# Attention with learned features beside a Mish feed-forward: weight loads rewritten and a new order of steps

## The chip, the cores and the metric

The kernel runs on one core of one Trainium2 chip. The metric is device time in microseconds (us): the median over runs of the whole kernel. A core has five engines with queues of their own: TensorE (PE, with its weight loads listed as PEld), VectorE (DVE), ScalarE (ACT), GpSimd (POOL) and SyncE (SP). SP issues nearly all transfers here, ACT a few; 16 DMA engines move them.

## The reference

```python
xn = layernorm(x)                                   # x: 1 x 2048 x 448, bf16
q, k, v = split(xn @ wqkv)                          # 16 heads of 28
phi(t) = concat(softmax(t @ w_phi), softmax(-(t @ w_phi)))   # per head, 28 x 28
kv, z = phi(k)^T v, sum over rows of phi(k)
o = (phi(q) kv) / (phi(q) z + 1e-6)
A = o @ wo
h = xn @ w1 + b1                                    # 448 to 1792
B = (h * tanh(softplus(h))) @ w2                    # Mish, then 1792 to 448
out = x + A + B
```

## The kernel before

The 2048 rows are held as 16 tiles of 128; two tiles make a pair `u` (0 to 7). The model width of 448 is three chunks of 128 and a tail of 64. For the tail the two tiles of a pair use the two halves of TensorE's rows at the same time: the normalised input is transposed to `xnT[u]` with the tail of the even tile on partitions 0 to 63 and that of the odd tile on 64 to 127. So each product has a part "F" (six matmuls over the full chunks, two tiles) and a part "H" (two matmuls of 64 rows, one per tile). The weights must therefore stand twice in their chunk 3, once in each half: `W1` (feed-forward) gets its tail by two transfers, `Wv` gets its by two, and `Wk` has its tail in partitions 0 to 63 and zeros (`p_wz`) in 64 to 127.

The feature map is folded into the projections: `Wp[1]` = Wk times w_phi and `Wp[0]` = Wq times w_phi. For this the key weights are transposed on TensorE (`w_tr`, steps wtk0 and wtk1; wtk1 holds the tail), the query weights by transposing transfers (`load_qT`, steps lqT0 to lqT3, with a doubling copy `qd`), and both are multiplied by the block-diagonal `Wbd` (`w_mm`, steps wmk and wmq). `Wbd` is built on GpSimd from the raw features `Wraw` and a 0/1 mask (`p_mask`, `w_bd`).

All work is a list of named steps. `ORDER` says in which order they are entered; each step appends its instructions to the queue of its engine, and each engine runs its own queue in that order, waiting only on what its instruction needs. Names that matter here, with `u` a pair, `t` a tile:

- `lx..`, `lkm`, `lkt`, `lvm`, `lvt`, `lp`, `lb`, `l1m`, `l1t`, `l2`, `lo`: loads of x, of key and value weights (main and tail), of features, bias, W1 (chunks and tail), W2 and Wo; the last letter is the queue (s for SP, a for ACT).
- `st` statistics (VectorE), `rt`/`rs` inverse deviation (ACT or GpSimd), `xm`/`xn` normalisation, `xa`/`xb` the transposition of a pair on TensorE in two parts (only pairs 3 and 1), `xt{u}m` the same by a transposing transfer on SP (the other pairs). An `xt` transfer waits until all of x is loaded.
- `v{u}`, `k{u}`, `q{u}` with F or H: the projections; `exk`, `exq` exponentials on ACT; `kn` and `qn` normalise the softmax (reduction on VectorE, multiplication on GpSimd); `kv{u}` the product of features and values, `kvz` its finish, `e{t}` transposing transfers of the query features.
- `f{half}.{c}` with F or H: first feed-forward product, followed by Mish on ACT; `g{t}` the second; `nd`, `ot`, `wo`, `sto` the attention output, its transposition, its projection and the stores.
- `z10`: ten matmuls on constants at the start.

Results of TensorE go to four pairs of PSUM banks; a pair is written again only when the engine that copies it out is done.

Of the kernel before, what the change touches and what calls it, by code (L numbers as in the profile page):

```python
# [35 lines left out]
def ap_on(src, dims):  # L36
    return bass.AP(tensor=src.tensor, offset=src.offset, ap=[list(src.ap[0])] + [list(d) for d in dims])
# [6 lines left out]
class Program:  # L44
# [46 lines left out]
    def dma(self, eng, fn, r=(), w=(), tag=""):  # L91
        return self.op(eng, fn, r, w, dma=True, tag=tag)
# [64 lines left out]
q5H xn7d k5H v4Ha k4H v4Fd qn6p xt7m l1m0s k4F qn4p q6F k6F v5Ha q6H qn7p qn2p k7H xt0m l1ts e7 k6H v5Fd kn3.0 k7F q7F  # L157
v6Fa q7H kn1.1 kn4.1 kn1.0 q0H qn13p f1.0H v6Ha q0F kn2.1 f1.0F f0.1F f0.5F v0Fd f0.1H f0.5H f1.2H kn3.1 v0Hd f1.2F
f1.5F f1.4H f1.5H k0H kn7.0 kn6.1 kn2.0 v7Hd kn7.1 ep f1.4F k0F v7Fd qn14p q4F f1.3F q4H kn5.1 e6 f0.2H f1.3H f0.0H
kn0.1 f0.2F f0.0F e2 f0.3F e4 kn6.0 kv7 e14 kn5.0 kn0.0 kv1 kv3 f0.9H f0.3H f0.9F los f1.1F kn4.0 f0.13F f0.10F f0.13H  # L160
f1.1H qn11p qn12p kv5 kv0 kv6 kv2 kv4 f0.12H f0.6H f0.10H f0.6F qn3p kvz qn9p f0.12F qn5p f1.6F e3 qn1p f1.6H qn8p
f0.4H f1.10H f0.7H qn0p f1.10F f0.4F nd7 wob e5 qn15p f0.7F nd4 f1.9F f0.11F f1.12F f0.11H f1.12H f1.8H f1.9H f1.8F
# [12 lines left out]
def _kernel(es, nc, A_x, A_wqkv, A_w_phi, A_wo, B_w1, B_b1, B_w2, out):  # L175
    def sb(name, shape, dtype):
        return es.enter_context(nc.sbuf_tensor(name, shape, dtype))
# [4 lines left out]
    ident = sb("ident", [P, P], BF16)  # L182
    mask = sb("mask", [GP, 4], FP32)
    Wraw = sb("Wraw", [GP, G, DH], BF16)
    Wbd = sb("Wbd", [GP, G, 2, 64], BF16)
    mask2 = sb("mask2", [P, 2, 2, DH], FP32)
    b1_rows = sb("b1_rows", [FC, P], BF16)
    b1T = sb("b1T", [P, FC], FP32)
# [50 lines left out]
    home_rows = {"Wk": [("Wk", 0), ("Wt", 0), ("Wt", 1), ("Wz",)], "Wv": [("Wv", 0)], "Wq": [("WqT", g) for g in range(G)] + [("WqTd",)],  # L239
                 "Wp1": [("Wp", 1, h, c) for h in range(2) for c in range(2)]}  # L240
# [22 lines left out]
    def pb(b):  # L263
        return ("ps", b)
# [14 lines left out]

    def load_tail(eng, name, dst, src):  # L280
        for i, (lo, hi) in enumerate(HALF):
            dma(eng, lambda e, lo=lo, hi=hi: e.dma_start(dst[lo:hi, 3, :], src[384:448, :]),
                w=[(name, 1 + i)], tag="ld" + name)

    def load_kv_tail(eng):
        dma(eng, lambda e: e.dma_start(Wkv[0:64, 3, :], A_wqkv[384:448, D:3 * D]), w=[("Wt", 0)], tag="ldWkt")  # L286
# [12 lines left out]
    def rows_of(name):  # L299
        if name in ("Wk", "Wv"):  # L300
            return [(name, 0), ("Wt", 0), ("Wz",) if name == "Wk" else ("Wt", 1)]
        return [("W1", 0, c) for c in range(3)] + [("W1", 1), ("W1", 2)]

    def load_phi(eng):
        dma(eng, lambda e: e.dma_start(Wraw[:], A_w_phi.rearrange("(g j) d f -> (j d) g f", j=4)), w=[("Wraw",)],
            tag="ldWphi")
# [27 lines left out]

    def p_mask():
        op("POOL", lambda e: e.memset(mask[:], 1.0), w=[("mask",)], tag="pm0")
        op("POOL", lambda e: e.affine_select(out=mask[:], in_=mask[:], compare_op=ALU.is_ge, fill=0.0, base=0,
                                             channel_multiplier=1, pattern=[[-DH, 4]]),
           r=[("mask",)], w=[("mask",)], tag="pm1")
        op("POOL", lambda e: e.affine_select(out=mask[:], in_=mask[:], compare_op=ALU.is_ge, fill=0.0, base=DH - 1,  # L340
                                             channel_multiplier=-1, pattern=[[DH, 4]]),
           r=[("mask",)], w=[("mask",)], tag="pm2")

    def p_wbd():
        op("POOL", lambda e: e.memset(Wbd[:], 0.0), w=[("Wbd0",)], tag="pw0")

    def p_wz():
        op("DVE", lambda e: e.memset(Wkv[64:128, 3, 0:D].bitcast(mybir.dt.uint32), 0), w=[("Wz",)], tag="pz0")

# [67 lines left out]
    def pe(fn, r, w, tag):  # L417
        return op("PE", fn, r=r, w=w, tag=tag)
# [173 lines left out]

    def w_bd():
        for r in range(2):
            op("POOL", lambda e, r=r: e.tensor_tensor(
                Wbd[:, :, r, 0:QP].rearrange("p g (j f) -> p g j f", f=DH),
                ap_on(Wraw[:, 0, 0:1], [[DH, G], [0, 2], [1, DH]]),
                ap_on(mask[:, 2 * r:2 * r + 1], [[0, G], [1, 2], [0, DH]]), ALU.mult),
               r=[("Wraw",), ("mask",), ("Wbd0",)], w=[("Wbd", r)], tag=f"Wbd{r}")

    def w_tr(h, eng):
# [27 lines left out]
    def w_mm(which, h, eng):  # L629
# [8 lines left out]
        def mm(e):  # L638
# [4 lines left out]
            return ins  # L643
        pe(mm, ([("WT", h), ("WU", h)] if which else [("WqT", g) for g in range(G)] + [("WqTd",)]) + [("Wbd", 0), ("Wbd", 1)], [pb(b), pb(b + 1)], f"wmm{which}{h}")
        if which and eng == "both":
# [120 lines left out]
    def bias_T():  # L766
        b = take1()
        pe(lambda e: e.transpose(bank16(b)[:, 0:FC], b1_rows[0:FC, :], ident[0:FC, 0:FC]), [("b1r",), ("ident",)],
           [pb(b)], "b1")
        evac("DVE", lambda: b1T[:], lambda: bank16(b)[:, 0:FC], [pb(b)], [("b1T",)], "b1e")  # L770

# [197 lines left out]
    add("table", table)  # L969
    add("bd", w_bd)  # L970
    for eng, c in (("SP", "s"), ("ACT", "a")):
        for name, a, b in (("x0", 0, 2), ("x1", 2, 4), ("x2", 4, 6), ("x3", 6, 8), ("x4", 8, 12), ("x6", 12, 16)):
            add(f"l{name}{c}", load_x, a, b, eng)
        for i, (n, t) in enumerate((("k", Wk), ("v", Wv))):
            add(f"l{n}m{c}", load_main, eng, "W" + n, t, A_wqkv[:, (i + 1) * D:(i + 2) * D])
        add(f"lkt{c}", load_kv_tail, eng)
        add(f"lvt{c}", load_v_tail, eng)
        for i in range(3):
            add(f"l1m{i}{c}", load_chunk, eng, "W1", W1, B_w1, i)
        add(f"l1t{c}", load_tail, eng, "W1", W1, B_w1)  # L980
        for name, fn in (("p", load_phi), ("b", load_b1), ("2", load_w2), ("o", load_wo)):
            add(f"l{name}{c}", fn, eng)
# [62 lines left out]
```

## Time and profile before

| | us |
|---|---|
| median of 3 runs (lowest, highest) | 152.07 (152.03, 152.78) |
| profiled execution | 151.9 |
| its span, first to last instruction | 150.4 |
| TensorE busy | 146.1 (97%) |
| VectorE / ACT / GpSimd busy | 90.3 / 71.4 / 70.4 |

Times inside the profile count from the first instruction of the profiled execution. A row of the chain is "start, duration, what"; a row of the timeline is "start, duration, engine, line, operation, output from input, count"; a row of transfers ends with the size of one transfer and the time from issue to landing. The windows list busy time of PE, PEld, DVE, ACT and POOL with counts, then the granted clock, the busy share of the 16 DMA engines and GB/s. Groups give total busy us and the mean ns of one instruction.

### The profile page before, as it was taken

To read this page: it belongs to the slowest core of one execution; us is meant where nothing else is said; L and a number is where in the kernel's file an instruction comes from. 1 tells how busy PE (TensorE), PEld (TensorE's weight loads), DVE (VectorE), ACT (ScalarE), POOL (GpSimd) and SP (SyncE) were. 2 spreads that over 40 slices of the span, in tenths; PEclk is the share of its full clock that TensorE was granted. 3 is DMA by queue.
4 is the path that set the end of the run, shared out by engine and by line. 5 is a ranking of instruction groups with operands and counts; after the bars stand their busy time and mean duration, and the time that the engine had idled before them with its cause. 6 is when DMAs were issued, how large, how long until landed. Compare 5 with 4: busy or idle time off the path is not lost.

```text
span 150.4 us, 2592 instructions
## 1 busy us (share of the span) xinstructions
PE 146.1 (97%) x1051; PEld 72.3 (48%) x1051; DVE 90.3 (60%) x180; ACT 71.4 (47%) x85; POOL 70.4 (47%) x77
## 2 busy tenths in 40 slices
PE   7899999999999999999999999999999999999992
PEld 2554444444443535454354445555455555554451
DVE  0997996899999899947986004514049351200641
ACT  3688998989986979546681974000000000000000
POOL 7522799399999999998999100000000000000000
PEclk9999999999999999999999999999999999999999
DMA  5997696796830009401479994530905933030206
GB/s 131 271 234 215 127 251 114 142 226 40 174 70 0 0 0 126 162 0 29 80 145 355 155 197 89 101 65 9 188 3 39 256 86 61 0 65 0 92 0 214
DMA packets 39480, 16.97 MB, mean 113 GB/s; under 512 B 33452, under 2 KB 38700, under 8 KB 39468
## 3 DMA queue, kind: packets, MB, share of 16 engines
q1 hardware_dynamic: 38860, 16.68, 51.6%
q10 hardware_dynamic: 608, 0.12, 0.4%
q8 instruction: 8, 0.13, 0.3%
q14 instruction: 4, 0.03, 0.1%
HBM read 6.97 MB, written 1.84 MB: 59 GB/s over the span
## 4 chain that ended last, share of the span: by engine, by line
PE 89%; SPq 5%; DMA 2%; DVE 1%; issue 0%
PE PS L440 49%; PE PS L883 28%; PE PS L899 7%; PE PS L800 2%; DMA WqT<-in_A_wqkv_dram 2%; SPq L292 2%; PE PS L707 2%; SPq L271 1%; SPq L274 1%; PE PS L641 1%; DVE x_all L848 0%; SPq L286 0%; SPq L289 0%; DVE WqT L296 0%; DVE x_all L869 0%
## 5 line engine op out<-in xcount | busy, mean ns | idle before, releaser
L440 PE MATMUL PS<-xnT,W 128*128 128x512 bf16 (+1 forms) x224 | 45.5, 379 | 0.0
L883 PE MATMUL PS<-W,actT 128*128 128x448 bf16 (+1 forms) x224 | 44.0, 351 | 0.0
L774 ACT ACTIVATE actT<-PS,b1T 128x1024 bf16<-128x1024 f32 x28 | 30.1, 1113 | 13.3 <-PE PS L440 13.1
L883 PEld LDWEIGHTS PS<-W,actT 128*128 128x128 bf16 x224 | 21.4, 98 | 18.8
L440 PEld LDWEIGHTS PS<-xnT,W 128*128 128x128 bf16 (+1 forms) x224 | 17.6, 97 | 24.4 <-issue 5.4
L755 POOL TENSOR_TENSOR EqS<-EqS,rSk 128x896 bf16<-128x896 bf16 x16 | 26.7, 1694 | 3.0 <-DVE rSk L753 3.0
L690 POOL TENSOR_TENSOR actT<-actT,rSk 128x896 bf16<-128x896 bf16 x16 | 26.6, 1693 | 0.0
L848 DVE TENSOR_TENSOR x_all<-PS,x_all 128x448 bf16<-128x448 f32 (+1 forms) x16 | 9.5, 617 | 20.8 <-PE PS L899 14.4
L805 DVE RECIPROCAL rden<-PS 128x16 f32<-128x16 f32 x16 | 4.0, 250 | 24.2 <-PE PS L800 24.2
L751 DVE TENSOR_REDUCE Sk<-EqS 128x32 f32<-128x896 bf16 x16 | 16.7, 1042 | 0.0
L686 DVE TENSOR_REDUCE Sk<-actT 128x32 f32<-128x896 bf16 x16 | 16.5, 1033 | 0.0
L740 ACT ACTIVATE EqS<-PS 128x896 bf16<-128x896 f32 x16 | 13.8, 943 | 2.6 <-PE PS L440 2.6
L678 ACT ACTIVATE actT<-PS 128x896 bf16<-128x896 f32 x16 | 13.7, 941 | 0.2 <-PE PS L440 0.2
L440 PE MATMUL PS<-Wkv,xnT 128*128 128x448 bf16 (+1 forms) x64 | 13.2, 353 | 0.0
L440 PE MATMUL PS<-Wpk,xnT 128*128 128x448 bf16 (+1 forms) x64 | 13.0, 353 | 0.0
L440 PE MATMUL PS<-Wpq,xnT 128*128 128x448 bf16 (+1 forms) x64 | 12.5, 353 | 0.0
L472 DVE BATCH_NORM_STATS2 stats<-x_all 128x6 f32<-128x448 bf16 x16 | 9.7, 608 | 2.6 <-DMA x_all<-in_A_x_dram 2.6
L807 DVE TENSOR_TENSOR xn<-PS,rden 128x448 bf16<-128x448 f32 x16 | 10.0, 625 | 0.6
L440 PEld LDWEIGHTS PS<-Wpq,xnT 128*128 128x128 bf16 (+1 forms) x64 | 5.2, 97 | 6.2 <-issue 1.9
L440 PEld LDWEIGHTS PS<-Wkv,xnT 128*128 128x128 bf16 (+1 forms) x64 | 5.0, 97 | 6.0 <-issue 1.9
L440 PEld LDWEIGHTS PS<-Wpk,xnT 128*128 128x128 bf16 (+1 forms) x64 | 5.3, 97 | 5.2 <-issue 0.6
L567 DVE CAST v_all<-PS 128x896 bf16<-128x896 f32 x5 | 5.4, 1079 | 2.3 <-PE PS L440 2.3
(80 smaller groups left out, 108.7 us busy)
## 6 DMA issues: line engine op xcount, KB each, us to landing
W<-in_B_w_dram SPq DMA_DIRECT2D x1, 1568.0 KB, 9.0
out_dram<-x_all SPq DMA_DIRECT2D x7, 224.0 KB, 2.3
W<-in_B_w_dram SPq DMA_DIRECT2D x3, 448.0 KB, 3.9
x_all<-in_A_x_dram SPq DMA_DIRECT2D x4, 224.0 KB, 3.5
x_all<-in_A_x_dram SPq DMA_DIRECT2D x2, 448.0 KB, 4.2
Wkv<-in_A_wqkv_dram SPq DMA_DIRECT2D x2, 336.0 KB, 4.1
Wo<-in_A_wo_dram SPq DMA_DIRECT2D x2, 336.0 KB, 4.0
W<-in_B_w_dram SPq DMA_DIRECT2D x2, 224.0 KB, 4.7
```

The lines of the kernel that those rows point to most:

```text
L440: ins = e.matmul(o, lhs(c, k), rhs(c, k), start=first and c in (0, 3), stop=not first and c in (2, 3))
L472: op("DVE", lambda e: e.bn_stats(stats[:, t, :], x_all[:, t, :]), r=[("x", t)], w=[("st", t)], tag=f"bn{t}")
L678: op("ACT", lambda e, s=s: e.activation(E_of(u)[:, s, :, :], two(b, D), ACT.Exp, scale=1.0 if s == 0 else -1.0), r=[pb(b), pb(b + 1)], w=[ ...
L686: op("DVE", lambda e: e.tensor_reduce(Sk[u][:, s, :], Eh(), AX.X, ALU.add), r=[("E", u, s)], w=[("Sk", u, s)], tag=f"Sk{u}.{s}")
L690: op("POOL", lambda e: e.tensor_tensor(Eh(), Eh(), ap_on(rSk[u][:, s, 0:1], [[1, 2 * H], [0, DH]]), ALU.mult), r=[("E", u, s), ("rSk", u, ...
L740: op("ACT", lambda e, s=s: e.activation(EqS[:, k:k + 2, :, s * QP:(s + 1) * QP], two(b, D).rearrange("p i (h n) -> p i h n", n=QP), ACT.Ex ...
L751: op("DVE", lambda e: e.tensor_reduce(ap_on(Sk[u][:, i, 0:1], [[4, 2 * G], [1, 4]]), E, AX.X, ALU.add), r=both, w=[("Sk", u, i)], tag=f"Sq ...
L755: op(eng, lambda e: e.tensor_tensor(E, E, ap_on(rSk[u][:, i, 0:1], [[4, 2 * G], [1, 4], [0, DH]]), ALU.mult), r=both + [("rSk", u, i)], w= ...
L774: op("ACT", lambda e: e.activation(actT[:, fc, q * 1024:(q + 1) * 1024], bank(b, 2), ACT.Mish, bias=b1T[:, fc:fc + 1]), r=[("b1T",), pb(b) ...
L807: op("DVE", lambda e: e.tensor_tensor(o_sb[u % NXN][:, i, :].rearrange("p (h d) -> p h d", d=DH), ap_on(bank(b)[:, 0:1], [[NC, H], [1, DH] ...
L883: ins = e.matmul(bank(b)[:, 0:width(t)], actT[:, fc, tok(t)], W2[:, fc, 0:width(t)], start=first and fc == 0, stop=last and fc == FC - 1)
L899: ins = e.matmul(bank(b)[:, 0:n], oT_of(u)[lo:hi, cc * P:(cc + 1) * P], Wo[lo:hi, cc, 0:n], start=first and c in (0, 3), stop=last and c i ...
```

## The change

- Features are loaded by four transfers on ACT (lp0 to lp3) directly into their blocks of `Wbd`; `Wraw`, the mask and `w_bd` go. The transfers wait for the memset of `Wbd`.
- The key tail goes into partitions 0 to 63 of `Wk`'s chunk 3 and the value tail into 64 to 127 of the same chunk, in one transfer of 128 rows; the zeros go. `Wv` keeps only the lower half of its own tail, and the products of odd tiles read the value tail from `Wk` (`tok_works` has a `W3`).
- The tail of `W1` is loaded in one transfer whose source names the same 64 rows twice.
- The bias is loaded by columns (`b1_cols`, 128 x 14), and the transposition on TensorE goes; a copy on VectorE makes it fp32.
- A new order. Among other things: x tiles 2 and 3 (lx1s) are loaded ahead of the value weights, tiles 4 and 5 last; wtk1b stands ahead of xa3a; tile 7 is normalised on GpSimd; the W1 tail (l1ts) is issued between xt5m and xt4m; nine constant matmuls instead of ten.

```diff
-pm pw lx3s pk pz lkms lkts lvms lvts lpa table pi lx1s lqT0 lx2s st6d rt6a st7d z10 rt7a lqT1 lx4s lqT2 lqT3 xm6d lx0s
-pv wtk0b lx6s xm7d xa3a wtk1b bd wmk0b xb3a st3d wmk1a st2d v3Fd st5d rt3p rt2a xm2d v3Ha xm3d lbs k3F st4d xa1a k3H
-xb1d v1Fa qd wmq1a rs2p st11d xn2d wmq0a st10d k1F b1 k1H st13d rs5p xn5p v1Ha q1H q3H st9d st12d q1F q3F xt2m q2F k2F
-st8d st0d k2H rs4p v2Hd st1d l1m1s xt5m xn4d rs6p rs0p l1m2s xt4m q2H xn6p st15d st14d v2Fd rs7p xt6m k5F xn0p q5F pp
...
+pw lx3s lkms lkts lx1s lvms lvts lx4s lp1a pi lp0a st6d lqT3 lp2a lqT0 lp3a st7d table rt6a z9 rt7a xm6d wtk0b xm7p
+wtk1b xa3a lqT1 st2d wmk0a rt2p lqT2 st3d xb3d lx0s pk rt3a wmk1a v3Fd xm2d xa1a v3Ha xm3d st10d st11d st8d qd st9d
+k3H rs5p xb1a lx6s k3F v1Fd xn5d lx2s wmq0a wmq1d rs4p v1Ha xn4p pp st15d k1H st14d st5d k1F xt5m l1ts q3F q1F st4d
+xt4m st1d st12d rs2p q1H xn2d rs7p kn1.0 q3H lbs v5Ha k5H k5F xt2m v5Fa q5F v4Fd st0d rs0p st13d xn7d l1m0s q5H rs6p
+v4Hd xn0d q4H q4F k2F xt7m k4F l1m1s pv xn6p k2H k4H v2Hd k7F kn1.1 v2Fa xt0m qn2p kn2.1 q2F xt6m kn4.0 kn2.0 k7H
...
-    def load_tail(eng, name, dst, src):
-        for i, (lo, hi) in enumerate(HALF):
-            dma(eng, lambda e, lo=lo, hi=hi: e.dma_start(dst[lo:hi, 3, :], src[384:448, :]),
-                w=[(name, 1 + i)], tag="ld" + name)
+    def load_w1_tail(eng):
+        src = bass.AP(tensor=B_w1.tensor, offset=B_w1.offset + 384 * F, ap=[[0, 2], [F, 64], [1, F]])
+        dma(eng, lambda e: e.dma_start(W1[:, 3, :], src), w=[("W1", 1)], tag="ldW1")
 
     def load_kv_tail(eng):
-        dma(eng, lambda e: e.dma_start(Wkv[0:64, 3, :], A_wqkv[384:448, D:3 * D]), w=[("Wt", 0)], tag="ldWkt")
+        src = bass.AP(tensor=A_wqkv.tensor, offset=A_wqkv.offset + 384 * 3 * D + D, ap=[[D, 2], [3 * D, 64], [1, D]])
+        dma(eng, lambda e: e.dma_start(Wk[:, 3, :], src), w=[("Wt", 0)], tag="ldWkt")
 
     def load_v_tail(eng):
-        dma(eng, lambda e: e.dma_start(Wkv[64:128, 3, D:2 * D], A_wqkv[384:448, 2 * D:3 * D]), w=[("Wt", 1)], tag="ldWvt")
+        dma(eng, lambda e: e.dma_start(Wv[0:64, 3, :], A_wqkv[384:448, 2 * D:3 * D]), w=[("Wt", 1)], tag="ldWvt")
...
-    def load_phi(eng):
-        dma(eng, lambda e: e.dma_start(Wraw[:], A_w_phi.rearrange("(g j) d f -> (j d) g f", j=4)), w=[("Wraw",)],
-            tag="ldWphi")
+    def load_phi(j, eng):
+        dma(eng, lambda e: e.dma_start(Wbd[j * DH:(j + 1) * DH, :, j // 2, j % 2 * DH:(j % 2 + 1) * DH],
+                                       A_w_phi.rearrange("(g j) d f -> j d g f", j=4)[j]),
+            r=[("Wbd0",)], w=[("Wbd", j)], tag=f"ldWphi{j}")
 
     def load_b1(eng):
-        dma(eng, lambda e: e.dma_start(b1_rows[:], B_b1.rearrange("(c p) -> c p", p=P)), w=[("b1r",)], tag="ldb1")
+        dma(eng, lambda e: e.dma_start(b1_cols[:], B_b1.rearrange("(c p) -> p c", p=P), allow_slow_non_contiguous=True), w=[("b1r",)], tag="ldb1")
...
-    def w_bd():
...
     def bias_T():
-        b = take1()
-        pe(lambda e: e.transpose(bank16(b)[:, 0:FC], b1_rows[0:FC, :], ident[0:FC, 0:FC]), [("b1r",), ("ident",)],
-           [pb(b)], "b1")
-        evac("DVE", lambda: b1T[:], lambda: bank16(b)[:, 0:FC], [pb(b)], [("b1T",)], "b1e")
+        op("DVE", lambda e: e.tensor_copy(b1T[:], b1_cols[:]), r=[("b1r",)], w=[("b1T",)], tag="b1e")
```

More of the change, by code (lines that the diff above doesn't have):

```diff
@@ L158 @@
[L158 to L162, printed above, removed]
@@ L167 @@
+nd12 wob g0 ot5m e0 g1 nd14 nd0 ot0m g13 ot7m wo5F ot6m g4 g12 g10 g14 wo7F wo6F wo0H wo7H wo6H wo5H wo0F sto6 g11
+sto2 sto0 sto3 g15 sto1 stt14 sto4 sto5 stt15
 """
@@ L182, in _kernel @@
     ident = sb("ident", [P, P], BF16)
-    mask = sb("mask", [GP, 4], FP32)
-    Wraw = sb("Wraw", [GP, G, DH], BF16)
     Wbd = sb("Wbd", [GP, G, 2, 64], BF16)
     mask2 = sb("mask2", [P, 2, 2, DH], FP32)
-    b1_rows = sb("b1_rows", [FC, P], BF16)
+    b1_cols = sb("b1_cols", [P, FC], BF16)
     b1T = sb("b1T", [P, FC], FP32)
@@ L238, in _kernel @@
     oT_home = [(Wkv, 0, ["Wk", "Wv"]), (Wkv, 14 * P, []), (WqT, 0, ["Wq"]), (Wp[1], 0, ["Wp1"])]
-    home_rows = {"Wk": [("Wk", 0), ("Wt", 0), ("Wt", 1), ("Wz",)], "Wv": [("Wv", 0)], "Wq": [("WqT", g) for g in range(G)] + [("WqTd",)],
+    home_rows = {"Wk": [("Wk", 0), ("Wt", 0), ("Wt", 1)], "Wv": [("Wv", 0)], "Wq": [("WqT", g) for g in range(G)] + [("WqTd",)],
                  "Wp1": [("Wp", 1, h, c) for h in range(2) for c in range(2)]}
@@ L333, in p_ident @@
            r=[("ident",)], w=[("ident",)], tag="pi1")
[L335 to L342, printed above, removed]
     def p_wbd():
         op("POOL", lambda e: e.memset(Wbd[:], 0.0), w=[("Wbd0",)], tag="pw0")
-    def p_wz():
-        op("DVE", lambda e: e.memset(Wkv[64:128, 3, 0:D].bitcast(mybir.dt.uint32), 0), w=[("Wz",)], tag="pz0")
     def p_ones():
@@ L589, in xT @@
              [("xnT", u), ("xnU", u)], f"xTe{u}")
-    def w_bd():
[L594 to L599, printed above, removed]
     def w_tr(h, eng):
@@ L643, in mm @@
             return ins
-        pe(mm, ([("WT", h), ("WU", h)] if which else [("WqT", g) for g in range(G)] + [("WqTd",)]) + [("Wbd", 0), ("Wbd", 1)], [pb(b), pb(b + 1)], f"wmm{which}{h}")
+        pe(mm, ([("WT", h), ("WU", h)] if which else [("WqT", g) for g in range(G)] + [("WqTd",)]) + [("Wbd", j) for j in range(4)], [pb(b), pb(b + 1)], f"wmm{which}{h}")
         if which and eng == "both":
@@ L662, in xchunk, with tok_works @@
         return c if c == 3 or par == 0 else 4 + c
-    def tok_works(u, W):
+    def tok_works(u, W, W3=None):
         return lambda b: [(bank(b + par)[:, 0:D], par,
                            lambda c, k, par=par: xnT[k[0]:k[1], u, xchunk(c, par), :],
-                           lambda c, k: W[k[0]:k[1], c, :]) for par in range(2)]
+                           lambda c, k, par=par: (W3 if W3 is not None and c == 3 and par else W)[k[0]:k[1], c, :])
+                          for par in range(2)]
     def v_mm(u, part, eng):
@@ L672, in then @@
                  [pb(b), pb(b + 1)], [("v", u)], f"ve{u}")
-        pair_part(f"v{u}", part, tok_works(u, Wv), [("xnT", u), ("xnU", u)] + rows_of("Wv"), then)
+        pair_part(f"v{u}", part, tok_works(u, Wv, Wk), [("xnT", u), ("xnU", u)] + rows_of("Wv"), then)
     def k_mm(u, part):
@@ L977, in _kernel @@
         add(f"lvt{c}", load_v_tail, eng)
+        for j in range(4):
+            add(f"lp{j}{c}", load_phi, j, eng)
         for i in range(3):
             add(f"l1m{i}{c}", load_chunk, eng, "W1", W1, B_w1, i)
-        add(f"l1t{c}", load_tail, eng, "W1", W1, B_w1)
-        for name, fn in (("p", load_phi), ("b", load_b1), ("2", load_w2), ("o", load_wo)):
+        add(f"l1t{c}", load_w1_tail, eng)
+        for name, fn in (("b", load_b1), ("2", load_w2), ("o", load_wo)):
             add(f"l{name}{c}", fn, eng)
@@ L987, in _kernel @@
     add("qd", double_qT)
-    for n, fn in (("pi", p_ident), ("pm", p_mask), ("pw", p_wbd), ("pz", p_wz), ("pv", p_ones), ("pk", p_mask2), ("pp", p_pads)):
+    for n, fn in (("pi", p_ident), ("pw", p_wbd), ("pv", p_ones), ("pk", p_mask2), ("pp", p_pads)):
         add(n, fn)
-    for n in (4, 8, 10, 12, 14, 16, 18, 20):
+    for n in (4, 8, 9, 10, 12, 14, 16, 18, 20):
         add(f"z{n}", warm, n)
```

17 lines of the change are left out of this document (9 added, 8 removed).

## The prediction

> **What bounds the kernel now.** I read the page first, then the chain in order of time, then TensorE's waits, the timeline, and last the DMA answers.
>
> ```profile
> PE 146.1 (97%) x1051; PEld 72.3 (48%) x1051; DVE 90.3 (60%) x180; ACT 71.4 (47%) x85; POOL 70.4 (47%) x77
> PE 89%; SPq 5%; DMA 2%; DVE 1%; issue 0%
> ```
> ```profile
> 1.25 0.41 SPq L274
> 1.72 0.56 SPq L286
> ...
> 8.97 3.54 DMA WqT<-in_A_wqkv_dram
> ...
> 14.98 0.16 PE PS L768
> 15.15 43.46 PE PS L440 x242
> ...
> 144.79 2.29 PE PS L883 x14
> ```
> ```profile
> PE PS L530 <- DVE xn L520: 0.2, 1, 0.2
> ```
>
> TensorE (PE) is the bound: 146.1 of 150.4 us, and from 15.15 us the chain is one row of matmuls behind another up to the last, at 147 us. In the waits only one row inside the work is left, 0.2 us. Two places can therefore move the time: the start, up to about 15.4 us, where PE waits for loads, and any later place where the new order makes PE wait. An edit on another engine after 15 us that makes PE wait nowhere is worth nothing.
>
> **What the trace says of how a load is spread.** The change rewrites five loads, so their price is the question.
>
> ```profile
> q1 hardware_dynamic: 38860, 16.68, 51.6%
> q10 hardware_dynamic: 608, 0.12, 0.4%
> Wraw<-in_A_w_phi_dram ACTq DMA_DIRECT2D x1, 24.5 KB, 3.1
> b_rows<-in_B_b_dram SPq DMA_DIRECT2D x1, 3.5 KB
> ```
>
> Queue q10 carries two loads of ACT: the feature weights (112 rows of 4 pieces, 448 packets) and the last store (128 rows). That makes 576; the other 32 of its 608 packets are 16 for each transfer, one closing packet from each of 16 engines. On q1 every transfer counts rows in multiples of 16 except the bias load with its 14 rows, and 38860 is 12 above a multiple of 16: 14 rows and 14 closing packets make 28, which is 16 + 12 (16 closing packets would leave 14). So the load whose outermost count is 14 ran on 14 engines, and it is also the one whose row has no landing time. [...]
>
> The two new 128-row loads read through a pattern whose outermost count is 2: the key tail `[[D, 2], [3 * D, 64], [1, D]]` and the feed-forward tail `[[0, 2], [F, 64], [1, F]]`. I take it that they run on 2 of 16 engines. How fast is one engine?
>
> ```profile
> 4.00:6.00 2.00, 1.65 (x15) 0.85 (x14) 1.93 (x7) 1.10 (x5) 1.85 (x6) 1.00 0.99 280
> 79.50:81.00 1.50, 1.50 (x9) 0.68 (x8) 1.50 (x2) 0.00 (x0) 1.50 (x2) 1.00 1.08 373
> ```
>
> The last two columns are the DMA share and GB/s. With all 16 engines full they move 280 (at the start) to 373 GB/s (the long load of W2, alone then): 17.5 to 23.3 GB/s for one. The key tail's 112 KB are 57 KB for each of two engines, 2.5 to 3.3 us, where 16 need 0.3 to 0.4. The feed-forward tail writes 448 KB, 229 KB for each of two: 9.8 us at the rate of the long load (13 at the other; its rows are long, so I take 9.8), where 16 need 1.2.
>
> [...]
>
> **The change, part by part.**
>
> *Start.* The second transposition of key weights, wtk1b, needs the key tail.
>
> ```profile
> Wkv<-in_A_wqkv_dram SPq DMA_DIRECT2D x1, 336.0 KB, 3.5
> Wkv<-in_A_wqkv_dram SPq DMA_DIRECT2D x1, 112.0 KB, 4.2
> ```
> ```profile
> 4.88 0.62 PE L612 MATMUL PS<-ident,Wkv 128*112 128x128 bf16 x8
> 5.93 0.65 PE L612 MATMUL PS<-ident,Wkv 128*112 128x128 bf16 x8
> 15.47 4.05 PE L440 MATMUL PS<-Wpq,xnT 64*128 64x448 bf16 x22
> ```
>
> Key weights issued at 1.25 land at 4.75; the tail issued at 1.72 lands at 5.9, and wtk1b starts at 5.93. With two engines it lands between 4.75 + 2.5 = 7.25 and 5.9 + 2.9 = 8.8; I take 7.8, so wtk1b starts 1.9 us later. Everything behind it on PE waits too, since the new order puts wtk1b ahead of xa3a. From wtk1b to the 15.47 us at which the four first units are done PE has 8.5 us of work (0.45 wtk1b, 0.4 + 0.4 + 0.8 for the products with the feature weights, 0.8 of input transposes, 4 units of 6 x 0.19 + 0.19 = 5.3, 0.4 of changes between full and half rows) in 9.54 us: 1.0 us of idle time that a late start can use up. Of this 0.2 is the bias transpose, now gone. The new order puts back about half: the second half of v3 waits for xb3d's copy, which on VectorE now stands behind both statistics of tiles 2 and 3 (4 instructions, 1.5 us, and those wait for x1, now loaded ahead of the value weights). So 1.9 - 0.5 = 1.4 later; ends 0.5 and 2.5.
>
> These parts of the start hide under that wait and I cost them at nothing:
>
> ```profile
> 0.81 0.40 ACTq L305 DMA_DIRECT2D Wraw<-in_A_w_phi_dram  x1
> 1.24 1.28 ACT L322 ACT_TABLE_LOAD   x1 [1.24 <-PEq L1030]
> 1.37 0.52 POOL L345 MEMSET Wbd<- 112x512 bf16 x1
> 4.33 0.29 POOL L331 TENSOR_SCALAR_AFFINE_SELECT ident<-ident 128x128 bf16<-128x128 bf16 x1
> 4.70 0.29 ACT L497 ACTIVATE lnv<-mv,eps_col 128x1 f32<-128x1 f32 x1 [2.17 <-POOL ident L331]
> 4.98 1.11 POOL L595 TENSOR_TENSOR Wbd<-Wraw,mask 112x224 bf16<-112x224 bf16 x2
> 16.45 1.73 POOL L547 TENSOR_SCALAR xn<-x_all,rstd,shift 128x448 bf16<-128x448 bf16 x3 [0.30 <-DVE shift L540]
> ```
>
> Four feature loads on ACT, 0.40 to 0.58 each, wait for the memset of Wbd (now POOL's first, done at 1.3) and end at 3.5; the table load behind them ends at 4.85, so the first logarithm moves from 4.70 to 4.87. The fourth load, issued at 2.95, lands at 6.05 by its row's 3.1; Wbd was ready at 6.09 before. POOL loses the mask and 1.11 us of w_bd, and ident comes at 2.2, which gains nothing since the key weights land at 4.75. Tile 7's normalisation on POOL costs about 1.0 (two of the three pieces of the last row), more than on VectorE. Without the late key tail these would cost 0 to 0.3 us. The query-weight transposes need to land by 14; on the two engines they are 2 us behind at worst (12.5 + 2), the same to 0.5.
>
> *Query evacuations, bias.* wmq1's two copies go from ACT to VectorE (no cost: the first q unit comes 0.3 us after them). The bias by columns is 128 x 14 pieces of 2 bytes, 1792 packets; 448 packets of the feature weights are the nearest row. It stands behind the transfer below, and the first Mish is after 40 us: nothing, at most 1 us of queue.
>
> *Row-mode changes.* Counted in both orders from the first q unit, changes between 128-row, 64-row and kv matmuls go from 32 to 31, each about 0.1 us: 0.1 less.
>
> *Feed-forward tail.* On SP it now stands between the input transposes of pairs 5 and 4.
>
> ```profile
> 14.98 1.27 SPq L572 DMA_TRANSPOSE xnT<-xn  x1
> 16.30 0.58 SPq L278 DMA_DIRECT2D W<-in_B_w_dram  x1
> 18.21 1.23 SPq L572 DMA_TRANSPOSE xnT<-xn  x1
> ```
> ```profile
> W<-in_B_w_dram SPq DMA_DIRECT2D x1, 448.0 KB, 3.9
> xnT<-xn SPq DMA_TRANSPOSE x1, 2.9
> ```
>
> Before, the same places held a W1 chunk of 448 KB at 16.30, landing in 3.9 us. xt5m needs the same load of x and tile pair 5, ready at about 15.2, so the tail is issued at 16.5. Of 3.9 us, 1.2 is data, so 2.7 is latency; the tail keeps its two engines until 16.5 + 2.7 + 9.8 = 29.0, counted to landing. xt4m, issued about 18.2, uses every engine and lies behind it on two; its own data adds 0.7 to 1.1: it lands at 29.7 to 30.1. PE needs it for v4F: q3 starts at 15.47 + 1.4 = 16.9, and q3, q1, v5, k5 and q5 before it are 6.6 us: due at 23.5. PE stands still for 6.2 us (ends 5 and 7). Nothing covers this: SP's queue is what PE waits for, xt2m, xt7m, xt0m, xt6m and three W1 chunks drain behind it at about 1.2 us each, and PE, as late, reaches each after it has landed. If the tail ran on 16 engines, xt4m would land at 21.5 and be covered by 2 us.
>
> *Clock.* After the standstill matmuls may run slow again:
>
> ```profile
> L440 PE MATMUL PS<-xnT,W 128*128 128x512 bf16 x168 | 38.5, 379 | 0.0
> L384 PE MATMUL PS<-const-bfloat16-1.0 128*128 128x512 bf16 x10 | 3.9, 567 | 0.8 <-PEq L1030 0.8
> ```
>
> The ten warming matmuls cost 3.9 us against 10 x 0.22 (38.5 / 168 is 0.23): 1.7 us lost after idleness. Ends 0 and 1.7; no row shows how long an idle gap must be, so I take 0.8. [...]
>
> *Rest.*
>
> ```profile
> L690 POOL TENSOR_TENSOR actT<-actT,rSk 128x896 bf16<-128x896 bf16 x16 | 26.6, 1693 | 0.0
> ```
>
> Later stages I went through wait by wait: POOL's 20 multiplications of 1.7 us before kv5 end about 1.5 us ahead of it, W2 and the Eq transposes come some us early, and the last g15 with its stores is as before. ACT runs close to PE from 26 to 45 us, and the standstill relieves it.
>
> **Sum.** 1.4 - 0.1 + 6.2 + 0.8 = 8.3. The profiled execution took 151.9 (150.4 span and 1.5 around it), 0.2 under the median of 152.07 of the runs. 151.9 + 8.3 = 160.2; I forecast 160.2.
>
> **Rivals.**
> - *The pair patterns are spread over 16 engines after all* (the count of two may be merged with the rows). Then the key tail lands by 6, q3 starts at 15.4, everything later is covered, but ACT, with exponentials back to back from 15.6 to 43 us and a table load, frees banks up to 0.5 us late at f0.2: 151.9 + 0.2 = 152.1 (151.4 to 152.9). For it: every load shown in before was spread wide. Against: the 14 closing packets.
> - *Faster.* As there, and the start also loses its 1.0 us of idle time, because x1 lands early:
>
> ```profile
> 3.48 0.58 SPq L271 DMA_DIRECT2D x_all<-in_A_x_dram  x1
> ```
> ```profile
> x_all<-in_A_x_dram SPq DMA_DIRECT2D x1, 224.0 KB, 4.2
> ```
>
>   It landed at 7.7; less 1.1 to 1.4 for the value weights' 392 KB, at about 6.5. Were tile 3's statistics through before xb3d's copy is wanted, q3 would start at 14.5: 151.9 - 1.0 - 0.1 = 150.8. It decides if the key tail lands before 6.0 and those statistics end by 7.7; by my reading of VectorE's queue they end at 8.5.
> - *Only the key tail hurts.* The feed-forward tail is not wanted before 40 us; if the transposes pass it instead of lying behind, 151.9 + 1.4 = 153.3. Against:
>
> ```profile
> 27.77 1.23 SPq L572 DMA_TRANSPOSE xnT<-xn  x1
> ```
> ```profile
> xnT<-xn SPq DMA_TRANSPOSE x1, 4.5
> ```
>
>   This one, issued 0.6 us behind a chunk of W1, landed after 4.5 us and not 2.9.
>
> **Chances.** Forecast 0.74, first rival 0.14, faster 0.05, only the key tail 0.07. The forecast's own range is 156 to 163 (start 0.5 to 2.5, standstill 5 to 7, clock 0 to 1.7, errors not all of one sign). That holds about 0.7 in all, so the range reaches down into the rivals, to 152. Within 0.5% of 152.07 (151.3 to 152.8), about what a measurement tells from no change: most of the first rival, 0.11; faster 0.05; slower 0.84.
>
> **What would show it.** The key tail's row lands at 7 to 9 us and wtk1b starts there; the feed-forward tail's row lands 12 us after issue, and while it runs the DMA share is near 2 of 16; PE's waits have a row of 5 us or more ending in xT of pair 4, between 23 and 30 us; q1's packets leave a remainder that fits two closers each for two loads. Wrong if both tails land in about 4 us: then the first rival, and the time is read from q3's start and from waits between 26 and 45 us.

## The result, and the profile after

| | before | after |
|---|---|---|
| median of the runs on one chip (us) | 152.05 | 164.48 |
| lowest, highest (4 runs each) | 151.96, 152.78 | 163.46, 164.57 |
| profiled execution, its span | 151.9, 150.4 | 164.43, 162.7 |
| TensorE busy | 146.1 (97%) | 150.3 (92%) |

The ratio is 1.0795 [1.0748, 1.0842]: the changed kernel is 12.4 us slower. That is 4.3 us more than the forecast of 160.2, and 1.5 above the upper end of its range. Line numbers in the rows below are those of the changed kernel (in the experiments they shift by one or two): L427 is the projections and the first feed-forward product (L440 before), L591 and L620 the key transposition and the product with the feature weights (L612 and L641 before), L559 the transposing transfers (L572 before), L280 the load of the W1 tail.

The page first: TensorE's busy time, the 40 slices of TensorE, of its granted clock and of the DMA engines, the two queues with their packets, and the chain's shares by engine.

```profile
PE 150.3 (92%) x1049; PEld 74.7 (46%) x1049; DVE 90.0 (55%) x180; ACT 72.2 (44%) x84; POOL 68.8 (42%) x71
PE   7499994099999999999999999999999999999994
PEclk9999999759999999999999999999999999999999
DMA  5996491695890000094539955947600600710066
q1 hardware_dynamic: 40660, 16.68, 53.8%
q10 hardware_dynamic: 648, 0.12, 0.4%
PE 84%; DMA 11%; DVE 2%; issue 1%; SPq 0%
```

Before, TensorE held 89% of the chain and DMA 2%; now DMA holds 11%. TensorE's slices show two holes, a shallow one in slice 2 (about 4 to 8 us) and a deep one in slices 7 and 8 (about 24 to 33 us), and in slices 8 and 9 the clock falls to 7 and 5 tenths. From slice 9 on, the row is as full as it was. Busy time grew by 4.2 us although two matmuls fewer ran: some of them ran slower.

TensorE's waits and the chain name the two holes:

```profile
PE PS L427 <- DMA xnT<-xn: 6.7, 1, 6.7
PE PS L591 <- DMA Wkv<-in_A_wqkv_dram: 2.4, 1, 2.4
```
```profile
1.71 6.57 DMA Wkv<-in_A_wqkv_dram
8.32 1.10 PE PS L591 x8
...
20.88 11.79 DMA xnT<-xn
32.66 0.14 issue
32.80 39.98 PE PS L427 x206
```

The key tail, issued at 1.7, lands at 8.28, and the second key transposition starts at 8.32 (5.93 before). The transpose of pair 4, issued by SP from 20.88, lands at 32.66, and TensorE waits 6.7 us for it. From 32.8 on the chain is one matmul behind another, as it was before.

What the DMA engines and SP did meanwhile (the answer on transfers for 15 to 34 us in 40 slices, and SP's timeline):

```profile
DMA  0001009990111119911111111111111799759998
GB/s 0 0 0 34 0 19 213 54 196 0 15 15 45 45 36 234 104 60 45 60 45 60 45 60 45 60 45 60 45 60 37 167 77 6 90 70 108 98 281 241
xnT<-xn SPq DMA_TRANSPOSE x4, 6.1
```
```profile
18.57 0.59 SPq L280 DMA_DIRECT2D W<-in_B_w_dram  x1
20.88 4.87 SPq L559 DMA_TRANSPOSE xnT<-xn  x1
...
26.43 4.95 SPq L559 DMA_TRANSPOSE xnT<-xn  x1
```

From 20 to 29.5 us, with one burst of other work in it, the busy share of the 16 engines is 1 tenth (0.13 from 26 to 28 us, as much as 2 of 16) and the rate mostly 45 to 60 GB/s: two engines at 22 to 30 each. And SP's next two transposes each hold SP itself for 4.9 us, where one took 1.2 before.

Last, TensorE's timeline and its windows (time, busy us of PE, granted clock, DMA share, GB/s):

```profile
4.83 1.07 PE L591 MATMUL PS<-ident,Wkv 128*112 128x128 bf16 x8
8.32 1.10 PE L591 MATMUL PS<-ident,Wkv 128*112 128x128 bf16 x8 [2.42 <-DMA Wkv<-in_A_wqkv_dram]
9.54 0.95 PE L620 MATMUL PS<-Wbd,EqS 112*128 112x112 bf16 x8
11.46 2.25 PE L427 MATMUL PS<-Wkv,xnT 128*128 128x448 bf16 x6
14.53 1.30 PE L427 MATMUL PS<-Wpk,xnT 128*128 128x448 bf16 x6
19.31 2.92 PE L427 MATMUL PS<-Wpq,xnT 128*128 128x448 bf16 x16
32.80 2.40 PE L427 MATMUL PS<-Wkv,xnT 128*128 128x448 bf16 x6 [6.68 <-DMA xnT<-xn]
...
37.94 2.92 PE L427 MATMUL PS<-Wpk,xnT 128*128 128x448 bf16 x16
```
```profile
29.00:30.00 1.00, 0.00 (x0) 1.00 0.19 54
30.00:31.00 1.00, 0.00 (x0) 0.72 1.39 95
31.00:32.80 1.80, 0.00 (x0) 0.50 0.80 82
32.80:36.00 3.20, 3.20 (x12) 0.50 1.16 213
37.00:37.50 0.50, 0.50 (x3) 0.73 0.88 351
37.50:38.00 0.50, 0.50 (x5) 1.00 0.30 115
```

The six matmuls of one F part (a "unit") take 1.30 us at 14.53, but 2.25 at 11.46 and 2.40 at 32.80. Behind the second wait the granted clock says why: it fell to 0.50 near 30.4, 4.3 us after TensorE stopped at 26.1, and came back near 37.3, 4.5 us after it started again. Behind the first wait the matmuls are as slow, from 8.3 to 13.5, but the clock column shows 1.00 there. The slow stretch does not begin with that wait: the first key transposition, at 4.83 and ahead of it, already took 1.07 us, where it took 0.62 before. And the column cannot be taken at its word so early: it reads 1.00 from the start, although the nine warming matmuls took 4.00 us, 0.44 each, and matmuls of that shape take 0.23 later.

### The profile page after: what moved, and what is told of

Its sections match the earlier page's. It is cut to its first block, busy times and chain, and to the rows that moved or that the text cites. A ratio compares the mean times of both kernels' runs of the same rounds, so it can differ in the third digit from the quotient of the medians.

```text
span 162.7 us, 2589 instructions
## 1 busy us (share of the span) xinstructions
PE 150.3 (92%) x1049; PEld 74.7 (46%) x1049; DVE 90.0 (55%) x180; ACT 72.2 (44%) x84; POOL 68.8 (42%) x71
## 3 DMA queue, kind: packets, MB, share of 16 engines
q1 hardware_dynamic: 40660, 16.68, 53.8%
## 4 chain that ended last, share of the span: by engine, by line
PE 84%; DMA 11%; DVE 2%; issue 1%; SPq 0%
PE PS L427 44%; PE PS L860 26%; DMA xnT<-xn 7%; PE PS L876 7%; DMA Wkv<-in_A_wqkv_dram 4%; PE PS L777 2%; PE PS L687 2%; PE PS L620 1%; DVE stats L459 1%; PE PS L517 1%; PE PS L591 1%; DVE Wpq L554 0%; DVE x_all L825 0%; SPq L272 0%; SPq L269 0%
## 5 line engine op out<-in xcount | busy, mean ns | idle before, releaser
L427 PE MATMUL PS<-xnT,W 128*128 128x512 bf16 (+1 forms) x224 | 45.4, 379 | 0.0
L860 PE MATMUL PS<-W,actT 128*128 128x448 bf16 (+1 forms) x224 | 43.3, 351 | 0.0
L427 PEld LDWEIGHTS PS<-xnT,W 128*128 128x128 bf16 (+1 forms) x224 | 17.7, 97 | 24.2 <-issue 5.0
L427 PE MATMUL PS<-Wkv,xnT 128*128 128x448 bf16 (+1 forms) x64 | 15.4, 399 | 6.7 <-DMA xnT<-xn 6.7
L427 PE MATMUL PS<-Wpq,xnT 128*128 128x448 bf16 (+1 forms) x64 | 13.4, 374 | 0.0
L427 PE MATMUL PS<-Wpk,xnT 128*128 128x448 bf16 (+1 forms) x64 | 12.3, 353 | 0.0
L427 PEld LDWEIGHTS PS<-Wkv,xnT 128*128 128x128 bf16 (+1 forms) x64 | 5.9, 106 | 13.5 <-issue 9.4
L554 DVE CAST v_all<-PS 128x896 bf16<-128x896 f32 x4 | 4.3, 1076 | 9.4 <-PE PS L427 9.4
L427 PEld LDWEIGHTS PS<-Wpq,xnT 128*128 128x128 bf16 (+1 forms) x64 | 5.3, 101 | 7.1 <-issue 3.3
```

The costliest lines, as they stand in the source:

```text
L427: ins = e.matmul(o, lhs(c, k), rhs(c, k), start=first and c in (0, 3), stop=not first and c in (2, 3))
L860: ins = e.matmul(bank(b)[:, 0:width(t)], actT[:, fc, tok(t)], W2[:, fc, 0:width(t)], start=first and fc == 0, stop=last and fc == FC - 1)
```

## The experiments

My theory after this profile: the two loads whose source has an outermost count of 2 run on two engines; the first delays the key transposition, the second stands ahead of the transpose of pair 4; and after each wait the clock costs more than I gave it. The rivals: the new order itself loses time, or the queue (not the load) is at fault, or the other rewritten loads share in it.

**1 and 2. One load at a time back to two halves.** First the W1 tail:

```diff
-        src = bass.AP(tensor=B_w1.tensor, offset=B_w1.offset + 384 * F, ap=[[0, 2], [F, 64], [1, F]])
-        dma(eng, lambda e: e.dma_start(W1[:, 3, :], src), w=[("W1", 1)], tag="ldW1")
+        for i, (lo, hi) in enumerate(HALF):
+            dma(eng, lambda e, lo=lo, hi=hi: e.dma_start(W1[lo:hi, 3, :], B_w1[384:448, :]), w=[("W1", 1 + i)], tag="ldW1")
```

> The changed kernel with one edit: the tail of W1 is loaded by two transfers of 64 rows instead of one of 128 whose source counts 2 outermost. Theory (a transfer whose source counts 2 outermost runs on two of 16 engines and holds up what is queued behind it): both halves land about 4 us after issue, the 6.7 us wait of TensorE for the transposed input of pair 4 goes, and with it the 2.1 us of half-speed matmuls behind it: 164.4 - 6.7 - 2.1 = 155.6 (155 to 156.5); q3 still starts near 19.3. Rival (the standstill comes from the new order on SyncE, or from the bias load in 1792 pieces, and not from this load): the wait stays above 4 us and the time above 161.

Measured: 154.48 us, ratio to before 1.0161 [1.0125, 1.0197], a little below the 155 to 156.5 that I expected. One wait for a load is left, that for the key tail; here is TensorE's timeline behind it:

```profile
8.20 0.65 PE L591 MATMUL PS<-ident,Wkv 128*112 128x128 bf16 x8 [2.38 <-DMA Wkv<-in_A_wqkv_dram]
...
9.01 0.55 PE L620 MATMUL PS<-Wbd,EqS 112*128 112x112 bf16 x8
...
10.20 2.44 PE L427 MATMUL PS<-Wkv,xnT 128*128 128x448 bf16 x6
...
13.75 1.30 PE L427 MATMUL PS<-Wpk,xnT 128*128 128x448 bf16 x6
```

The wait is the same as in the changed kernel, and here too a unit takes 2.44 us instead of 1.30 for a while, though not right behind the wait: the transpositions there run at full rate. In this run the granted clock shows the slow stretch: its mean is 0.989 over a span of 153.2 us, as much as 3.4 us at 0.50, and the matmuls are slow from 9.8 to 13.2 us, beginning 4.0 us after TensorE stopped at 5.8. The first q unit starts at 18.54.

Then the key tail alone:

```diff
-        src = bass.AP(..., offset=A_wqkv.offset + 384 * 3 * D + D, ap=[[D, 2], [3 * D, 64], [1, D]])
-        dma(eng, lambda e: e.dma_start(Wk[:, 3, :], src), w=[("Wt", 0)], tag="ldWkt")
+        for i, (lo, hi) in enumerate(HALF):
+            dma(eng, lambda e, i=i, lo=lo, hi=hi: e.dma_start(Wk[lo:hi, 3, :], A_wqkv[384:448, (1 + i) * D:(2 + i) * D]),
+                w=[("Wt", 2 * i)], tag="ldWkt")
```

> The changed kernel with the other tail edited: the key and value tail of Wk's chunk 3 comes by two transfers of 64 rows. Theory: the second key transposition starts near 6 instead of 8.3, the matmuls from there on run at full speed (48 to 57 ns apart instead of 93 to 107), and q3 starts at 15.4 to 16 instead of 19.3. The W1 tail is issued only about 2 us earlier, so TensorE's wait for pair 4 grows to about 8 and the time falls only to about 162 (161 to 163). Rival (the new order, wtk1b ahead of xa3a and the statistics ahead of xb3d's copy, makes the start slow by itself): q3 starts after 17.5 and the time stays within 1 us of 164.4.

Measured: 163.02 us, ratio 1.0722 [1.0685, 1.0759], the upper end of what I expected. This kernel's wait for a transpose and its first q unit:

```profile
PE PS L428 <- DMA xnT<-xn: 8.8, 1, 8.8
```
```profile
15.28 2.92 PE L428 MATMUL PS<-Wpq,xnT 128*128 128x448 bf16 x16
```

With the key tail in halves the first q unit starts at 15.28 and not 19.31, as early as before the change (15.47). Of the 4 us gained there 2.1 are lost again to a longer wait (8.8 instead of 6.7), since TensorE comes earlier to the late transpose, and 0.6 to a longer stretch of half clock (5.8 us instead of 5.1 from the restart to the next k unit; the window from 35 to 36 us still reads 0.50). So most of the price is the W1 tail's.

**3. Both in halves**, all else of the change kept, the new order too.

> The changed kernel with both tails loaded by two transfers of 64 rows each; features, bias and order stay as changed. Theory: nothing is left but the order: 152.1 (151.4 to 152.9), q3 near 15.4, no wait of TensorE above 0.7 us. Rival (features in four transfers, bias in 1792 pieces or the order cost some us by themselves): above 154, with a wait that names which.

Measured: 152.54 us, ratio 1.0031 [1.0012, 1.0050]. Three short waits remain (0.8 for a transpose, a little over the 0.7 that I expected at most):

```profile
PE PS L428 <- DMA xnT<-xn: 0.8, 1, 0.8
PE PS L518 <- POOL xn L504: 0.5, 1, 0.5
PE PS L592 <- DMA Wkv<-in_A_wqkv_dram: 0.4, 1, 0.4
```

Against this kernel the slow key tail alone costs 154.48 - 152.54 = 1.9 us, the slow W1 tail alone 163.02 - 152.54 = 10.5, both together 11.9. New order, feature loads, bias by columns and second rows cost 152.54 - 151.96 = 0.6 us between them. That settles the first and the last rival.

**4. The clock.** Both slow loads stay; constant matmuls fill the two waits.

```diff
-... xm6d wtk0b xm7p
+... xm6d wtk0b z6 xm7p
-... v5Fa q5F v4Fd ...
+... v5Fa q5F z24 v4Fd ...
```

> The changed kernel with both slow tails kept, and matmuls on constants put where TensorE waits: 6 behind wtk0b, 24 behind q5F (their results are not used). Theory (half of what the sum missed is the clock, which falls when TensorE is idle): the matmuls from wtk1b to v3F run 48 to 57 and 189 ns apart instead of 93 to 107 and 373, those behind the wait 189 instead of 364; the transfers end no earlier than before by more than 1.5 us, so 164.4 - 2.1 - (0 to 1.5) = 160.8 to 162.3. Rival (the matmuls are slow for another reason, such as the transfers writing memory beside them): the spacing stays and the time stays within 0.7 us of 164.4.

Measured: 161.15 us, ratio 1.0599 [1.0562, 1.0635]; mean granted clock 1.000 (0.979 before the fillers). Its timeline at the same places:

```profile
8.35 0.65 PE L591 MATMUL PS<-ident,Wkv 128*112 128x128 bf16 x8 [0.75 <-DMA Wkv<-in_A_wqkv_dram]
9.18 0.55 PE L620 MATMUL PS<-Wbd,EqS 112*128 112x112 bf16 x8
17.69 2.92 PE L427 MATMUL PS<-Wpq,xnT 128*128 128x448 bf16 x16
31.44 1.30 PE L427 MATMUL PS<-Wkv,xnT 128*128 128x448 bf16 x6 [1.70 <-DMA xnT<-xn]
...
34.49 1.68 PE L427 MATMUL PS<-Wpk,xnT 128*128 128x448 bf16 x8
```

The key tail lands as late as ever (8.35), yet the eight transpositions behind it take 0.65 and not 1.10, the product with the feature weights 0.55 and not 0.95, and the first q unit starts at 17.69 and not 19.31: 1.6 us of the start were clock. This share differs between executions: run 1, with the same wait, has 18.54 there, 0.9 us of it. After the second wait the first unit takes 1.30 and not 2.40, and the four parts from there to the next k unit take 34.49 - 31.44 = 3.05 where they took 37.94 - 32.80 = 5.14: 2.1 us more of clock. In this kernel idleness thus costs 1.6 + 2.1 = 3.7 us beyond the waits themselves. The late transpose comes 1.4 us sooner (31.44 for 32.80), so 1.4 + 2.1 = 3.5 of it can reach the end; 3.3 did.

**5, 6, 9. Is it the load or its place?** Both runs have the key tail in halves. Run 5 keeps the slow W1 tail but issues it behind the last W1 chunk; run 6 has two halves at that place.

```diff
-... k1F xt5m l1ts q3F ...        ... l1m2s los ...
+... k1F xt5m q3F ...             ... l1m2s l1ts los ...
```

> Edit: the changed kernel with the key tail in two halves (as in the second run); the W1 tail stays one load with the doubled source, so it still moves on two engines for about 10 us, but it is issued behind the last W1 chunk (near 30 us) and not between the transposes of pairs 5 and 4. Theory (the price is the place in the queue: the load itself is slow but nobody wants it before the first feed-forward tail product near 48.5 us): it lands 30.3 + about 12.5 = 43, no wait at all behind it but the Wo loads and the first query-feature transposes, which are wanted after 60 us. The wait for xT of pair 4 goes altogether, since that transpose is now issued at 16.2 and due at 22: third run's 152.5 less 0.8 = 151.7, range 151.2 to 152.3. Rival (two engines blocked for 10 us cost time wherever the load stands, through the transfers behind it): 153 or more, with a PE wait on W1, Wo or EqS after 40 us.

> Edit: as the run before it, but the W1 tail as two loads of 64 rows, at the same late place. Theory (place alone): the same time as the run before it within 0.3%, 151.7 (151.2 to 152.3). Rival (the doubled source costs time by itself): the run before it is 1 us or more slower than this one.

Measured: run 5 157.68 us, 1.0351 [1.0306, 1.0395], well outside what I expected; run 6 151.91 us, 0.9978 [0.9953, 1.0003]. In run 5 TensorE stood still once more, before the first feed-forward unit:

```profile
29.76 0.65 SPq L280 DMA_DIRECT2D W<-in_B_w_dram  x1
```
```profile
43.06 10.59 PE L428 MATMUL PS<-xnT,W 128*128 128x512 bf16 x38 [4.04 <-issue]
```

My due time was wrong: I had read 48.5 off the first group of 64-row matmuls in the timeline, but a group there merges shapes, and in the program each F part, too, waits for all rows of W1 (`rows_of`), so the due time was 39.0. "issue" says that the profile found no releaser. Run 9 tells whether it was the load: it is run 5's kernel, but the F parts wait only for the three chunks that they read:

```diff
-                  rows_of("W1") + [(n, u) for u in ...
+                  rows_of("W1")[:3 if part == "F" else 4] + [(n, u) for u in ...
```

> Edit: the fifth run's kernel (key tail in halves, the W1 tail one load with the doubled source, issued near 29.8 us behind the last W1 chunk), and the F parts of the first feed-forward product wait only for the three chunks they read, not for all of W1 as before; the H parts still wait for the tail. The fifth run had shown the load landing 13.3 us after its issue, at 43.06, with the first F part wanting all of W1 at 39.0 (my expectation there had taken the due time from the first 64-row group of the timeline, 48.5). Theory (the load costs only what it is late where it is wanted): F parts start at 39.0 again; the first H part comes 12 matmuls of 0.22 us later, at 41.7, so PE waits 1.4 us at most for a landing at 43.1 and keeps its clock: sixth run's 151.9 + 1.4 = 153.3, range 152.0 to 153.8. Rival (something else behind the load, Wo or EqS, held PE up): 156 or more as in the fifth run.

```profile
PE PS L428 <- DMA W<-in_B_w_dram: 1.3, 1, 1.3
```
```profile
38.80 2.75 PE L428 MATMUL PS<-xnT,W 128*128 128x512 bf16 x12
42.90 5.03 PE L428 MATMUL PS<-xnT,W 64*128 64x512 bf16 x26 [1.34 <-DMA W<-in_B_w_dram]
```

Measured: 152.65 us, 1.0020 [0.9996, 1.0043]. Twelve matmuls run at 38.80, and the wait for the tail is 1.3 us. So the same slow load costs about 10 us in the changed kernel's place (run 2 against run 3), 5.8 in run 5's and 0.7 here (both against run 6); what it cost here is only how much too late it, or what it held up, came. The four Wo loads and the transposes of query features behind it held nobody up.

**7. A better version?** Run 6 with the bias load behind the last W1 chunk and tile 7 on VectorE again.

> Edit: as the run before it, and two more: the bias load goes behind the last W1 chunk (so its 1792 pieces are not ahead of the transpose of pair 2), and tile 7 is normalised on VectorE, as in the kernel before, not on GpSimd. Theory: the third run's wait of 0.5 us for GpSimd's xn in the second half of pair 3's input transposes goes: 151.7 - 0.5 = 151.2 (150.8 to 151.7), 0.5% under the kernel before. Rival: VectorE's 0.4 us more delays the statistics of tiles 2 and 3, a wait for xb3's copy takes its place, and the time stays at 151.7.

Measured: 151.88 us, 0.9986 [0.9969, 1.0004], the same as run 6: the rival's outcome. Run 6's own profile had no wait for GpSimd any more, but one of 0.6 us for ACT's copy just ahead of that place; in run 7 one for VectorE's copy stands just behind it, as the rival has it:

```profile
PE PS L428 <- DVE xnT L555: 0.3, 1, 0.3
```

Neither run 6 nor run 7 can be told from the kernel before. No version that beats it was found.

**8. One part alone on the kernel before.** Its two W1 tail loads become the one with the doubled source, in their old place behind the last input transpose.

> Edit on the kernel before, one part alone: its two W1 tail loads become the one load with the doubled source, in their old place behind the last input transpose (29.04 us). Theory: issued near 29.1, landed about 12.5 later, 41.6; here the first feed-forward tail product is due at 36.19, so PE waits about 5.4 us for W1 itself, then about 2 us of half clock: 152.0 + 7.4 = 159.4, range 157.5 to 160.5. Rival (the load is only slow because other transfers stand around it; alone at this place it lands in 6 to 7 us as the two halves would): 152 to 152.5, no wait.

Measured: 159.66 us, 1.0498 [1.0464, 1.0532], as the theory had it. Its wait and the packets of its main queue:

```profile
PE PS L439 <- issue: 5.2, 1, 5.2
```
```profile
q1 hardware_dynamic: 38830, 16.68, 53.1%
```

The load was issued at 29.43, and TensorE went on at 42.14, 12.7 us later. The profile names no releaser here either; what the matmul there still wants is W1's tail. The last W1 chunk was issued 1.9 us ahead of it and no load of W1 or Wo followed, and from 39 to 41 us the DMA share was 0.12 to 0.13: two engines were busy with it alone, and it was as slow. The queue has 30 packets fewer than before the edit (38860): two loads with 16 closing packets each have become one with 32 - 30 = 2.

**10. Does another queue help?** Run 2's kernel with the slow tail issued by ACT.

```diff
-... k1F xt5m l1ts q3F ...
+... k1F xt5m l1ta q3F ...
```

> Edit: the second run's kernel (key tail in halves, W1 tail one load with the doubled source, between the transposes of pairs 5 and 4), but the tail is issued by ACT and so goes through ACT's queue, not SP's. Theory A (what holds the transposes is the order within SP's queue): with the tail in another queue the transposes of pairs 4, 2 and 7 pass it, share two engines with it and land at most 2 us later than in the sixth run; PE waits 1 us or less before 35 us; the tail lands by 31, long before 39: 152.4, range 151.8 to 153.8. Theory B (each of the two engines works off whatever reached it, in order of arrival, whichever queue it came by): a transpose issued behind it lands at 29 us or later; the transpose of pair 4 may slip out ahead of it, then pair 2, due at 24.9, is late by 4 to 6 us and SP's issues still take near 5 us: 157 to 162.

Measured: 160.63 us, 1.0507 [1.0429, 1.0584]: theory B. The answer on transfers for 15 to 30 us and SP's timeline:

```profile
q1 hardware_dynamic: 4114, 0.59, 106.0%
q10 hardware_dynamic: 130, 0.46, 8.5%
```
```profile
20.64 9.35 SPq L560 DMA_TRANSPOSE xnT<-xn  x1
```
```profile
PE PS L428 <- DMA xnT<-xn: 7.1, 1, 7.1
```

In ACT's queue the tail was alone: 130 packets, its 128 rows and 2 closers. They took 8.5% of 16 engines over 15 us, 20.4 us of engine time, 10.2 on each of two. And SP's queue, which the tail was not in, waits as before: the transpose of pair 4 is 7.1 us late and the next holds SP for 9.35. So in this run it was the two engines that were shared, not the queue.

## Why the prediction was right or wrong

The mechanism, its two places and the sign were right; the size was 4.3 us short, and the step of the prediction that failed is *Clock*. By term:

| term | predicted | shown |
|---|---|---|
| start, late key tail without clock | +1.4 | +2.2 |
| row-mode changes | -0.1 | not separable |
| standstill for the transpose of pair 4 | +6.2 | +6.7 |
| clock | +0.8 | +3.7 |
| sum | +8.3 | +12.6 (12.4 measured) |

*Premise.* Right, though no row of before has a load with a count of 2: that the two loads would run on two engines was an estimate from the one load with 14. The runs showed it: 40660 packets are 4 above a multiple of 16, the two closers of each of two loads (before, 12 above), and runs 8 and 10 count 2 for one load directly. The rate of one engine was taken from full-load rows at 17.5 to 23.3 GB/s; 10.2 us for 229 KB (run 10) is 22.5, and the 9.8 us of data were 10.2. The four feature loads, which count 28 outermost, ran on 14 engines each: q10's 648 packets are 576 of data and 72 closers, 16 of the store and 14 of each load. So here a count of 28, above 16, did not bring all 16 engines. And one transfer of 128 rows with a count of 2 in place of two halves was the slower choice for the W1 tail: two halves 152.54 (run 3), one 163.02 (run 2).

*Start.* Wrong by +0.8. Of it 0.5 is the landing (8.28 instead of 7.8); the rest is idle time that was not won back, 0.2 and not 0.5. The end of 2.5 held. Run 4 is the basis: 17.69 - 15.47 = 2.2 with the clock kept up.

*Feed-forward tail.* Nearly right, by two errors that cancel. The tail was issued at 18.57 and not 16.5, since SP's transpose of pair 5 came later with the late start, so the transpose of pair 4 landed at 32.66 and not 29.7; but PE was due at 26.1 and not 23.5. The wait, 6.7, lies in the stated ends.

*Clock.* Wrong, and the reason the time left the range. I split a loss of 1.7 us, read off the warming matmuls, in half for want of a row, and only after the standstill. Run 4 shows 2.1 there, more than the stated end of 1.7: in the changed kernel the clock fell to 0.50 after 4.3 us of idle time and returned only 4.5 us after the restart. And it shows 1.6 at the start, around a wait of 2.4 us, a place for which the prediction had no clock term at all. Its sum for the start took all matmuls at full rate, but in the changed kernel they were slow when the wait began (1.07 for the first key transposition, 0.62 before) and stayed so up to 13.5; with matmuls in the wait they were fast behind it. Nine warming matmuls instead of ten are not the cause by themselves: runs 2 and 3 have nine too, and their first q unit comes at 15.28 and 15.16. How long an idle gap must be, the runs show only in part: the wait of 6.7 us brought half clock, that of 1.3 in run 9 none (mean clock 1.000), and behind the 2.4 us wait of run 1 the matmuls ran slow for 3.4 us (mean 0.989); the changed kernel's own first wait tells nothing on this, as its matmuls were slow before it.

*Costed at nothing.* Features, ACT's table, the bias by columns, GpSimd's work for tile 7, query evacuations and later stages: together with the order they cost 0.6 in run 3, where three waits stand (0.8 for a transpose behind the two W1 loads, 0.5 for GpSimd's tile, 0.4 for the key weights; in run 9 the product with the feature weights also waits 0.7 for a feature load), and nothing that can be told in run 6, with the W1 loads moved back (151.91). I had foreseen 0 to 0.3 without the late key tail, so this was fair.

*Rivals.* "Only the key tail hurts" is refuted in this place (run 2), but run 9 shows where it is true: a load nobody stands behind. "Faster" fails for another cause than I gave: with both tails in halves the first q unit starts at 15.16 (run 3), 0.3 sooner, not 14.5; what TensorE waits for ahead of it there are GpSimd's tile 7 and the key weights, not the statistics of tiles 2 and 3.

*What would show it.* The signs came: key tail at 8.28, a DMA share near 2 of 16, a wait of over 5 us for pair 4's transpose (it ended at 32.8, not by 30), the remainder of q1. No row of the changed kernel has the landing of the feed-forward tail; in run 8 it came 12.7 us after the issue, in run 9 13.2.

## What to carry to other kernels

Look at the outermost count of a transfer's source before merging two loads into one: here the merged load with a count of 2 took 12.7 us from issue until TensorE went on (run 8), where the two halves landed in 4.7 before. The closing packets of a queue, its total modulo 16, told here how many engines moved it (2 of 130 packets in run 10). Price a slow load by what is wanted behind it on the same engines, and read due times from the program's waits, not from merged timeline groups. When a wait of some us opens on TensorE, add the slow matmuls around it as a term of its own: here 3.7 us on top of 9.1 us of waiting, while 1.3 us of waiting in run 9 cost no clock.

## What was not expected of the hardware

- With a load on two engines under way, the engine that issued the next transfers was held up too: SP 4.9 us by each transpose behind it, and 9.35 us by one when the slow load was in ACT's queue (run 10), against 1.2 before.
- The granted clock fell to 0.50 some 4.3 us after TensorE stopped (26.1 to 30.4) and rose some 4.5 us after the restart (32.8 to 37.3). The work behind it paid 2.1 us. The delay differed between runs: by the window means the clock fell 3.2 us after the stop in run 5 (0.92 over 38 to 43.06 us) and 4.8 in run 8 (0.81 over 41 to 42.1), and it stayed at 0.50 for 6.8 us here, for 3.4 in runs 1 and 8.
- Around the 2.4 us wait at the start, matmuls ran at half rate from the first on until 13.5 us while the clock column showed 1.00; six filler matmuls in the wait removed what lay behind it. In run 1, with the same wait, they were fast behind it (0.65) and then slow from 9.8 to 13.2, with a mean granted clock of 0.989. Why one execution took the first course and the other the second stays open.
